# Banded attention followed by a ReLU-squared FFN on one core: earlier first load, other load order, pair-mask copies moved behind block 3

## Chip, cores, metric

The kernel runs on one core of one Trainium2 chip. The metric is the device time of one execution in microseconds; lower is better. All runs told here are of the state called fast; the kernel uses one core, so a slow die plays no part.

The names of the engines: PE is TensorE (PEld its loads of weights), DVE is VectorE, ACT ScalarE, POOL GpSimd and SP SyncE. "Clock" below is the share of PE's full clock that the trace shows as granted. A load "lands" when its data are on the chip.

## The reference, cut to what matters

```python
# q, k, v: (batch 8, heads 8, seq 576, head_dim 64) float32
scores = scale * q @ k.T                        # per batch and head
mask   = (rel >= 0) & (rel < 128)               # causal window of 128
scores = where(mask, scores + slope[h] * -abs(rel), -1e9)
attn   = softmax(scores);  a = attn @ v
x = a as (4608 tokens, 512)
h = x @ w_in                                    # 512 x 2048
out = maximum(h, 0) ** 2 @ w_out                # 2048 x 512
```

The 576 positions of a batch are cut into five blocks, four of 128 and one of 64 tokens, so there are 40 blocks, b0 to b39. A block's scores need its own keys and those of the block before it. 512 tokens make one FFN group, so group 0 is b0 to b3.

## The kernel before

The kernel is a planner. Each operation is added as a task with an engine, a sort key and its dependencies; the planner simulates the engines with rough durations and emits the instructions in the order that it finds. So moving one task can move others on all engines. On the chip each engine then works through its own list in that order.

The parts that the change touches are these; cuts are marked.

```python
FIRST = "b0 b1 b2 i0 i1 i2 b3 i3 o0 b4 b5 o1 b6 b7 o2 o3 b8 b9"   # order of loads: b block, i quarter of w_in, o quarter of w_out
KQ_PE = [0, 1, 2, 3, 4, 5, 6, 7, 8, 9]      # blocks whose k and q are transposed on PE; the others by DMA
WARM = 24                                    # dummy matmuls at the very beginning
FILL, UNTIL = 0.8, 26e3                      # share of planned PE gaps filled with dummy matmuls
...
t_iota = plan.add({"POOL": 360.0}, -9.1e5, build_iota)            # first on POOL, ahead of all loads
def build_ident():
    nc.vector.tensor_single_scalar(ident32, dist[:, 1], 0.0, op=ALU.is_equal)
    nc.vector.tensor_copy(ident, ident32)
...                                          # dist (DVE), then 8 masks (ACT)
def pair_rest():
    nc.vector.tensor_copy(pair_masks[:, :, 0:128].rearrange(...), masks[:, :, :, 0:64])
def pair_own():
    nc.vector.tensor_copy(pair_masks[:, :, 128:256], masks[:, :, 1, :])
t_pair = [plan.add({"DVE": 340.0}, -9e5 + 9, f, later + t_mask) for f in (pair_rest, pair_own)]
...
def load(key, ns, emit, deps=(), acq=()):
    return plan.add({"POOL": 900.0}, key, emit, deps, acq, dma=ns)   # issued by POOL, float32 in HBM to bf16 on chip
def load_w_in(n, key):                       # one quarter of w_in: 1 MB read, 512 KB written
    def emit():
        w = d_ff // 4
        nc.gpsimd.dma_start(w_in_sb[:, :, n * w:(n + 1) * w], moe_w_in[:, n * w:(n + 1) * w].rearrange(...))
    t_win[n] = load(key, 2550.0, emit)
...                                          # block 0's k and q: float32 through SP's queue; all else through POOL
```

The pair masks serve the bursts in which a 64-token block is taken together with the first block of the next batch; block 4 is the first of them. The dummy matmuls ("fillers") are there to keep PE busy, and so its clock up. Iota writes the table of distances from which the masks are built.

The softmax here doesn't subtract the row's maximum and nothing guards it: scores larger than these inputs give would overflow.

Of the kernel before, what the change touches and what calls it, by code (L numbers as in the profile page):

```python
# [38 lines left out]
class Plan:  # L39


    LAT = {"PE": 260.0, "ACT": 220.0, "DVE": 220.0, "POOL": 200.0, "SP": 2200.0}
    BEGIN = {"POOL": 1250.0}

    def __init__(self, bufs, pools, cold):
        self.tasks = []
# [124 lines left out]
def kernel(  # L171
    ctx: ExitStack, tc: tile.TileContext, q, k, v, moe_w_in, moe_w_out, out
):
    nc = tc.nc
# [12 lines left out]
    NG = NT // 512  # L187
    NBLK = B * NKB

    FIRST = "b0 b1 b2 i0 i1 i2 b3 i3 o0 b4 b5 o1 b6 b7 o2 o3 b8 b9"  # L190
    SPLIT = {0: [(0, 128), (128, 256), (256, 384), (384, 512)], 1: [(0, 192), (192, 512)]}
    EARLY = -80
    AHEAD = {10: -60, 1: 60, 4: 90, 9: -60, 5: -60, 0: -30, 12: 60, 11: 90, 2: 60, 8: 90, 7: 60, 6: 0, 3: -30, 24: 30, 14: 0, 18: 30, 25: 0, 23: 30, 16: -30, 13: 30, 21: 0, 19: -30}
    LEAD = 20

    KQ_PE = [0, 1, 2, 3, 4, 5, 6, 7, 8, 9]
    X_PE = [0, 1, 2, 3, 4, 5, 7, 8, 12, 17]
    WARM = 24
    FILL, UNTIL = 0.8, 26e3
    COLD = 0  # L200
    BANKS = {"A": 4, "B": 4}
    HOLD, OSB = 12, 14

# [17 lines left out]
        return [const.tile(shape, BF16, name=f"{name}_{i}") for i in range(n)]  # L221


    size = {"kq": 8, "v": 8, "kqT": 5, "P": 2, "x": 4}
    kq = ring("kq", size["kq"], [128, 2, d_model])
    vt = ring("vt", size["v"], [128, H, D + 1])
    kqT = ring("kqT", size["kqT"], [128, 2 * C, 128])
# [14 lines left out]


    def build_iota():
        nc.gpsimd.iota(dist, pattern=[[-128, 2], [1, 128]], base=128, channel_multiplier=-1,
                       allow_small_or_imprecise_dtypes=True)

    t_iota = plan.add({"POOL": 360.0}, -9.1e5, build_iota)

    def build_ident():  # L250
        nc.vector.tensor_single_scalar(ident32, dist[:, 1], 0.0, op=ALU.is_equal)
        nc.vector.tensor_copy(ident, ident32)

    t_ident = plan.add({"DVE": 350.0}, -9e5 - 1, build_ident, [t_iota])

    def build_dist():
        mid = (window - 1) / 2.0
# [16 lines left out]
                                 scale=-(2.0 ** (-8.0 * (h + 1) / H)))  # L274
        t_mask.append(plan.add({"ACT": act(256)}, -9e5 + h, build_mask, [t_dist]))

    later = []

    def pair_rest():
        nc.vector.tensor_copy(pair_masks[:, :, 0:128].rearrange("p h (t s) -> p h t s", t=2), masks[:, :, :, 0:64])  # L280

    def pair_own():
        nc.vector.tensor_copy(pair_masks[:, :, 128:256], masks[:, :, 1, :])  # L283

    t_pair = [plan.add({"DVE": 340.0}, -9e5 + 9, f, later + t_mask) for f in (pair_rest, pair_own)]

    def ones():
        nc.vector.memset(zero, 0.0)
# [26 lines left out]
    def load(key, ns, emit, deps=(), acq=()):  # L315
        return plan.add({"POOL": 900.0}, key, emit, deps, acq, dma=ns)

    t_win = [None] * 4
    t_wout = [None] * 4

    def load_w_in(n, key):
        def emit():
            w = d_ff // 4
            nc.gpsimd.dma_start(
                w_in_sb[:, :, n * w:(n + 1) * w],
                moe_w_in[:, n * w:(n + 1) * w].rearrange("(c p) f -> p c f", p=128))
        t_win[n] = load(key, 2550.0, emit)

    def load_w_out(n, key):
        def emit():  # L330
# [7 lines left out]
    def load_block(m, key):  # L338
        b, kb = divmod(m, NKB)
        n = blk[kb]  # L340
        wide = m == 0
        s_in[m, "k"] = s_in[m, "q"] = Slot("kq")
        s_in[m, "v"] = Slot("v")
        for i, (nm, src) in enumerate((("k", k), ("q", q), ("v", v))):
            sl = s_in[m, nm]
            if wide and nm != "v":
                def emit32(i=i, src=src):
                    nc.sync.dma_start(kq32[:, i].rearrange("s (h d) -> s h d", h=H),
                                      src[b, :, kb * 128:kb * 128 + n, :].rearrange("h s d -> s h d"))
                t_in[m, nm] = plan.add({"SP": 450.0}, key + 0.01 * i, emit32, dma=870.0)  # L350
                continue

            def emit(i=i, src=src, sl=sl, nm=nm):
                o = (vt[sl.idx][0:n, :, 0:D] if nm == "v"
                     else kq[sl.idx][0:n, i].rearrange("s (h d) -> s h d", h=H))
                nc.gpsimd.dma_start(o, src[b, :, kb * 128:kb * 128 + n, :].rearrange("h s d -> s h d"))  # L356
            deps = [t_ones] if nm == "v" else []
            if n < 128:
                deps.append(t_zeros.get("v" if nm == "v" else "kq"))
            t_in[m, nm] = load(key + 0.01 * i, 870.0 * n / 128, emit, deps, [sl])  # L360

    for i, what in enumerate(FIRST.split()):
        {"b": load_block, "i": load_w_in, "o": load_w_out}[what[0]](int(what[1:]), -9e5 + i)
# [24 lines left out]
    def turn(m):  # L388
# [12 lines left out]
        elif m == 0:  # L401
            t_kq = []
            for i in range(2):
                slot = Slot("B")
                last = None
                for c in range(C):
                    def emit(i=i, c=c, slot=slot):
                        nc.tensor.transpose(bank(slot)[:, c * 128:(c + 1) * 128],
                                            kq32[:, i, c * 128:(c + 1) * 128], ident32)
                    last = plan.add({"PE": mm(128)}, due - 56, emit,  # L410
                                    [last, t_ident, t_in[m, "kq"[i]]] + chain["tp"],
                                    ([slot] + ([sk] if i == 0 else [])) if c == 0 else [])
                chain["tp"] = [last]

                def evac(i=i, slot=slot):
                    copy(t_kq[i], kqT[sk.idx][:, i * C:(i + 1) * C, 0:n],
                         slot.tile.rearrange("p (c s) -> p c s", c=C)[:, :, 0:n])
                t_kq.append(plan.add({"ACT": act(C * n), "DVE": dve(C * n)}, due - 56, evac, [last], [], [slot]))
        else:
            slot = Slot("B" if first else "A")  # L420
            slot.turns = True
            last = None
            for i in range(2 * C):
                def emit(i=i):
                    nc.tensor.transpose(bank(slot)[:, i * 128:(i + 1) * 128],  # L425
                                        kq[s_in[m, "k"].idx][:, i // C, (i % C) * 128:(i % C + 1) * 128], ident)
                last = plan.add({"PE": mm(128)}, due - 56, emit,
                                [last, t_ident, t_in[m, "kq"[i // C]]] + ([t_in[m, "q"]] + chain["tp"] if i == 0 else []),
                                [slot, sk] if i == 0 else [], [s_in[m, "k"]] if i == 2 * C - 1 else [])
            chain["tp"] = [last]  # L430
            t_kq = []
            for i in range(2):
                def evac(i=i):
                    copy(t_kq[i], kqT[sk.idx][:, i * C:(i + 1) * C, 0:n],
                         slot.tile[:, i * 512:(i + 1) * 512].rearrange("p (c s) -> p c s", c=C)[:, :, 0:n])
                t_kq.append(plan.add(both if first else {("DVE", "ACT")[i]: both[("DVE", "ACT")[i]]},
                                     due - 56, evac, [last], [], [slot]))
# [3 lines left out]
    def score(ms):  # L441
# [6 lines left out]
        for i, m in enumerate(ms):  # L448
# [1 line left out]
            parts_of[m] = ([(0, m - 1)] if kb else []) + [(1, m)]  # L450
            P_of[m] = (sP, t_P)
            for part, mk in parts_of[m]:
                at = 128 * i + 64 * part if pair and i == 0 else 128 * part
                at_of[m, part] = at
                rel = [sk_of[mk]] if part == 0 or kb == NKB - 1 else []
                work_of.append((m, mk, n, at, rel))
        lo = min(w[3] for w in work_of)
        hi = max(w[3] + w[2] for w in work_of)
        n = 128 if pair else work_of[0][2]

        def burst():

            for sl in slot_s:
                bank(sl)
            for c in range(C):
                for m, mk, w, at, _ in work_of:
                    for half in range(2):
                        rows = slice(half * 64, half * 64 + 64)
# [2 lines left out]
                                :, c % 2, at:at + w],  # L471
                            kqT[sk_of[mk].idx][rows, c, :], kqT[sk_of[m].idx][rows, C + c, 0:w],
                            start=True, stop=True)
        tm = plan.add({"PE": 220.0 + C * sum(max(w[2], 64) / 2.4 + 4 for w in work_of)}, due - 28, burst,
                      [t for w in work_of for x in w[:2] for t in t_kq_of[x]] + chain["s"], slot_s + [sP],
                      [x for w in work_of for x in w[4]])
        chain["s"] = [tm]
        for i in range(4):
            def view(t):
                if pair:  # L480
                    return t
                return t.rearrange("p c (t q) -> p c t q", t=2)[:, :, lo // 128:2, 0:n]

            def Pv(i=i):
                return view(Pt[sP.idx][:, 2 * i:2 * i + 2].rearrange("p h t q -> p h (t q)"))

            def expo(i=i):
                nc.scalar.activation(Pv(i), view(slot_s[i].tile.rearrange("p (c x) -> p c x", c=2)),  # L488
                                     AF.Exp, bias=0.0, scale=scale)
            cols = 2 * sum(w[2] for w in work_of)  # L490
            te = plan.add({"ACT": act(cols)}, due - 28 + 3 * i, expo, [tm], [], [slot_s[i]])

            def mask(i=i):
                pt = Pv(i)
# [79 lines left out]
    while m < NBLK:  # L574
        ms = [m, m + 1] if m % NKB == NKB - 1 and m + 1 < NBLK else [m]
        for x in ms:
            turn(x)
        score(ms)
        for x in ms:
            mix(x)  # L580
        m += len(ms)
# [8 lines left out]
    def fc_step(g, unit, key, lo=0, hi=512):  # L590
# [10 lines left out]
        for fi, fc in enumerate(fcs):  # L601
            for cc in range(C):
                def emit(cc=cc, fc=fc, fi=fi):
                    nc.tensor.matmul(bank(slot)[:, fi * w:(fi + 1) * w], w_in_sb[:, cc, fc * 128:(fc + 1) * 128],  # L604
                                     xT[:, cc, g * 512 + lo:g * 512 + hi], start=cc == 0, stop=cc == C - 1)
                last = plan.add({"PE": mm(w)}, key + (fi * C + cc) * w / 512, emit,
                                [last, t_win[fc // 4]] + tokens(g * 512 + lo, g * 512 + hi),
                                [slot, sg] if cc == 0 and fi == 0 else [])
        srt = Slot("rt")

# [90 lines left out]
    def filler(slot, n):  # L701
        def emit():
            for i in range(n):
                if slot.turns:
                    nc.tensor.transpose(bank(slot)[:, 0:128], zero, ident)
                else:
                    nc.tensor.matmul(bank(slot)[:, 0:128], zero, zero, start=True, stop=True)  # L707
        t = Task({"PE": 107.0 * n / 2}, 0, emit, [t_ones, t_ident], [slot])
        t.eng, t.start, t.end, t.seq, t.cols = "PE", 0.0, 0.0, 0, 128 * n
        return t  # L710

# [47 lines left out]
```

## Time and profile before

The median was 312.97 us (312.77 to 313.3, 3 runs).

| reading | value | where |
|---|---|---|
| span | 311.3 us | page |
| chain that ended last, on PE | 95% | page, part 4 |
| first FFN matmul | 16.27 us | timeline |
| masks on ACT | 6.93 to 9.48 us | timeline |
| pair-mask copies on DVE | 9.52 to 11.07 us | timeline |
| quarter 0 of w_in lands | 14.8 us | DMA view (issue plus time to landing) |

From the page of the kernel before, its engine totals and its chain (part 4 gives shares of the span by engine, then by engine, tile and line):

```profile
PE 303.2 (97%) x2784; PEld 174.2 (56%) x2824; DVE 165.3 (53%) x482; ACT 179.2 (58%) x342; POOL 107.3 (34%) x134
...
PE 95%; ACT 1%; DVE 1%; issue 1%; DVEq 0%
PE B L604 40%; PE B L665 40%; PE A L469 6%; PE A L516 5%; PE A L311 1%; PE B L516 1%; ACT masks L273 1%; PE B L707 1%; PE A L425 1%; ACT kqT L375 1%; PE B L425 0%; DVE kqT L373 0%; PE A L562 0%; PE B L562 0%; DVE pair_masks L283 0%
```

L604 and L665 are the two FFN products. PE is the limit nearly everywhere, so the kernel is as long as the lost time at its begin plus PE's work. A caution: the page has 812 of 832 matmuls of L604 and 572 of 592 of L665, by the count of weight loads. PE looks idle where a record is missing, so the small idle times after 35 us are no real waits.

The timeline of the kernel before, single lines of the first 17 us (start, duration, engine, line, what, and in brackets the idle time before it and who ended that):

```profile
0.84 0.34 POOL L245 IOTA dist<- 128x256 f32 x1 [0.39 <-POOLq L743]
1.38 1.04 POOL L356 DMA_DIRECT2D vt<-in_v_dram  x1 [0.19 <-DVE vt L290]
...
5.34 1.06 PE L408 MATMUL B<-ident,kq 128*128 128x128 f32 x4
...
6.93 2.55 ACT L273 ACTIVATE masks<-dist 128x256 bf16<-128x256 f32 x8
7.63 2.31 POOL L324 DMA_DIRECT2D w_in_sb<-in_moe_w_in_dram  x3
...
9.52 0.67 DVE L280 COPY pair_masks<-masks 128x1024 bf16<-128x1024 bf16 x1 [1.14 <-ACT masks L273]
10.11 0.96 DVE L283 COPY pair_masks<-masks 128x1024 bf16<-128x1024 bf16 x1
...
16.27 1.06 PE L604 MATMUL B<-xT,w_in_sb 128*128 128x128 bf16 x16
```

The reader sees two things run side by side: the chain on chip (masks, pair copies, scores, softmax, x) and the queue of loads on POOL. The first FFN matmul needs both. When quarter 0 of w_in lands is read from the DMA view, restricted to the stretch in which it was issued (7.63 us); its last column is the time from issue to landing:

```profile
w_in_sb<-in_moe_w_in_dram POOLq DMA_DIRECT2D x1, 512.0 KB, 7.2
```

7.63 + 7.2 = 14.8 us. So in this execution the data waited about 1.4 us for the chain, not the chain for the data.

Up to about 7 us its PE works at half its later pace: block 0's k transposes take 1.06 us at 5.34 us. In the trace of e10_small_before (an experiment below, with the same instructions up to there) they are faster:

```profile
4.98 0.61 PE L408 MATMUL B<-ident,kq 128*128 128x128 f32 x4
```

In e8_extra_before, too, they took 0.61 us, at 5.28 us. The first FFN matmul was at 15.38 us in e10_small_before, and in e8_extra_before PE was free for it from 15.8 us. So up to 0.9 us of the 16.27 us, and of the slack of 1.4 us, belongs to this one execution. The clock column does not show it: it reads 1.00 from 1 to 8 us in all three traces.

### The profile page before, as it was taken

What the parts mean: (1) busy time and instruction counts of PE and PEld (TensorE: products, weight loads), DVE (VectorE), ACT (ScalarE), POOL (GpSimd) and SP (SyncE); (2) the same over time, 40 slices, a digit from 0 to 9 for tenths busy, and PEclk for the clock granted to TensorE, in tenths of its full rate; (3) what the DMA queues carried; (4) which work ended last, traced back from release to release, by engine and by line L of the source; (5) the groups of instructions that cost most, each with busy time, mean ns of one, the idle gap of its engine ahead of it and who ended that gap; (6) DMA issues with size and microseconds to landing.
All of it is one profiled execution on the core that took longest, in us unless ns stands there. A gap on an engine that the chain in (4) does not pass through costs nothing.

```text
span 311.3 us, 7139 instructions
## 1 busy us (share of the span) xinstructions
PE 303.2 (97%) x2784; PEld 174.2 (56%) x2824; DVE 165.3 (53%) x482; ACT 179.2 (58%) x342; POOL 107.3 (34%) x134
## 2 busy tenths in 40 slices
PE   8899999999999999999999999999999999999996
PEld 8799868675555555455454544445444454444443
DVE  4777666566557867676265555556455542222200
ACT  3777747585467847666455656665456654444411
POOL 8845958885546184365532120100000000000100
PEclk9999999999999999999999999999999999999999
DMA  9999999999999999999999994755422120000021
GB/s 133 181 190 179 173 181 158 167 156 149 148 147 164 144 115 153 134 171 151 210 180 165 134 200 118 137 127 103 128 87 84 53 59 34 37 34 35 34 97 73
DMA packets 168114, 39.86 MB, mean 128 GB/s; under 512 B 159440, under 2 KB 163792, under 8 KB 168080
## 3 DMA queue, kind: packets, MB, share of 16 engines
q0 software_dynamic: 114896, 18.88, 88.1%
q1 hardware_dynamic: 53184, 20.52, 33.5%
q8 instruction: 22, 0.36, 0.5%
q14 instruction: 12, 0.10, 0.1%
HBM read 36.70 MB, written 9.44 MB: 148 GB/s over the span
## 4 chain that ended last, share of the span: by engine, by line
PE 95%; ACT 1%; DVE 1%; issue 1%; DVEq 0%
PE B L604 40%; PE B L665 40%; PE A L469 6%; PE A L516 5%; PE A L311 1%; PE B L516 1%; ACT masks L273 1%; PE B L707 1%; PE A L425 1%; ACT kqT L375 1%; PE B L425 0%; DVE kqT L373 0%; PE A L562 0%; PE B L562 0%; DVE pair_masks L283 0%
## 5 line engine op out<-in xcount | busy, mean ns | idle before, releaser
L604 PE MATMUL B<-xT,w_in_sb 128*128 128x512 bf16 (+3 forms) x812 | 144.5, 312 | 1.7 <-issue 0.8
L665 PE MATMUL B<-w_out_sb,g 128*128 128x512 bf16 (+2 forms) x572 | 141.4, 373 | 1.3 <-issue 0.5
L613 ACT ACTIVATE rt<-B 128x512 bf16<-128x512 f32 (+2 forms) x152 | 86.6, 583 | 73.4 <-PE B L604 67.2
L620 DVE TENSOR_TENSOR g<-rt 128x512 bf16<-128x512 bf16 (+2 forms) x152 | 61.3, 406 | 73.5 <-ACT rt L613 72.4
L604 PEld LDWEIGHTS <-w_in_sb 128*128 128x128 bf16 x832 | 66.7, 98 | 48.0
L665 PEld LDWEIGHTS <-g 128*128 128x128 bf16 x592 | 54.2, 98 | 55.9
L488 ACT ACTIVATE P<-A 128x512 bf16<-128x512 f32 (+1 forms) x132 | 69.4, 589 | 19.2 <-PE A L469 19.2
L496 DVE TENSOR_TENSOR P<-P,masks 128x512 bf16<-128x512 bf16 (+1 forms) x104 | 42.4, 412 | 25.7 <-ACT P L488 22.3
L356 POOL DMA_DIRECT2D vt<-in_v_dram x40 | 34.3, 859 | 46.2 <-PE A L516 43.2
L356 POOL DMA_DIRECT2D kq<-in_k_dram x39 | 33.5, 859 | 44.7 <-DMA kqT<-kq 38.4
L356 POOL DMA_DIRECT2D kq<-in_q_dram x39 | 33.5, 860 | 6.5 <-DMA w_in_sb<-in_moe_w_in_dram 1.8
L636 ACT ACTIVATE osb<-B 128x512 f32<-128x512 f32 (+1 forms) x36 | 21.6, 600 | 23.9 <-PE B L665 23.9
L516 PEld LDWEIGHTS <-P 128*128 128x128 bf16 x576 | 26.8, 98 | 14.8 <-DVE P L496 0.5
L644 POOL DMA_DIRECT2D out_dram<-osb x3 | 1.7, 563 | 89.5 <-ACT osb L636 89.5
L544 DVE TENSOR_TENSOR x<-A,rec 128x256 bf16<-128x256 f32 (+1 forms) x70 | 28.8, 419 | 1.4
L516 PE MATMUL A<-vt,P 128*128 128x65 bf16 x504 | 25.7, 193 | 0.0
L469 PEld LDWEIGHTS <-kqT 64*128 64x128 bf16 x576 | 14.9, 94 | 12.9 <-issue 12.2
L469 PE MATMUL A<-kqT,kqT 64*128 64x128 bf16 (+1 forms) x256 | 17.8, 212 | 0.9 <-DVE kqT L373 0.8
L469 PE MATMUL A<-kqT 64*128 64x128 bf16 (+1 forms) x320 | 18.4, 211 | 0.0
L539 DVE RECIPROCAL rec<-A 128x4 f32<-128x4 f32 (+1 forms) x70 | 12.1, 179 | 11.6 <-PE A L516 10.8
L496 DVE TENSOR_TENSOR P<-P,pair_masks 128x512 bf16<-128x512 bf16 x28 | 11.7, 420 | 6.7 <-ACT P L488 5.6
L638 DVE COPY osb<-B 128x128 f32<-128x128 f32 x1 | 0.3, 291 | 13.7 <-PE B L665 13.7
(48 smaller groups left out, 82.6 us busy)
## 6 DMA issues: line engine op xcount, KB each, us to landing
out_dram<-osb SPq DMA_DIRECT2D x32, 256.0 KB, 2.3
vt<-in_v_dram POOLq DMA_DIRECT2D x32, 128.0 KB, 6.1
kq<-in_k_dram POOLq DMA_DIRECT2D x31, 128.0 KB, 6.2
kq<-in_q_dram POOLq DMA_DIRECT2D x31, 128.0 KB, 6.5
w_in_sb<-in_moe_w_in_dram POOLq DMA_DIRECT2D x4, 512.0 KB, 9.9
w_out_sb<-in_moe_w_out_dram POOLq DMA_DIRECT2D x4, 512.0 KB, 9.1
out_dram<-osb POOLq DMA_DIRECT2D x3, 256.0 KB, 2.4
kq<-in_k_dram POOLq DMA_DIRECT2D x8, 64.0 KB, 6.8
```

Source lines behind the costliest of these rows:

```text
L356: nc.gpsimd.dma_start(o, src[b, :, kb * 128:kb * 128 + n, :].rearrange("h s d -> s h d"))
L469: nc.tensor.matmul(slot_s[2 * (c // 2) + half].tile.rearrange("p (c x) -> p c x", c=2)[:, c % 2, at:at + w], kqT[sk_of[mk].idx][rows, c, : ...
L488: nc.scalar.activation(Pv(i), view(slot_s[i].tile.rearrange("p (c x) -> p c x", c=2)), AF.Exp, bias=0.0, scale=scale)
L496: nc.vector.tensor_tensor(pt, pt, view(mk), op=ALU.mult)
L516: nc.tensor.matmul(bank(slot_v)[:, hi * (D + 1):(hi + 1) * (D + 1)], Pt[sP.idx][:, place(h)].rearrange("p t q -> p (t q)")[:, at_of[m, par ...
L539: nc.vector.reciprocal(srec.tile[0:n, :], pv[0:n, :, D])
L544: nc.vector.tensor_tensor(xt[sx.idx][0:n, hf * 256:(hf + 1) * 256].rearrange("p (h e) -> p h e", h=4), pv[0:n, :, 0:D], srec.tile[0:n, :]. ...
L604: nc.tensor.matmul(bank(slot)[:, fi * w:(fi + 1) * w], w_in_sb[:, cc, fc * 128:(fc + 1) * 128], xT[:, cc, g * 512 + lo:g * 512 + hi], star ...
L613: nc.scalar.activation(srt.tile[:, 0:cols], slot.tile[:, 0:cols], AF.Relu, bias=0.0, scale=1.0)
L620: nc.vector.tensor_tensor(sg.tile[:, fcs[0]:fcs[-1] + 1, lo:hi], r, r, op=ALU.mult)
L636: nc.scalar.activation(so.tile[:, lo:hi], slot.tile[:, lo:hi], AF.Copy)
L665: nc.tensor.matmul(bank(slot)[:, lo:hi], sg.tile[:, fc, t * 128:(t + 1) * 128], w_out_sb[:, fc, lo:hi], start=fc == 0, stop=fc == FCB - 1)
```

## The change

Its intent is to begin dense PE work earlier. A load goes ahead of iota; block 1's k and q go ahead of block 0's v; the pair-mask copies leave the begin and follow block 3's mask multiplies; the second quarter of w_in comes as two loads (so i0 to i4 are five loads, and i4 is the last quarter); block 4 is loaded ahead of the last quarter of w_in. Besides: half the fillers, four more warm-up matmuls, block 9's k and q transposed by DMA instead of PE, one kq, one v and one x buffer fewer, other priorities. The code for "quarters" is new too but switched off (99).

```diff
-    FIRST = "b0 b1 b2 i0 i1 i2 b3 i3 o0 b4 b5 o1 b6 b7 o2 o3 b8 b9"
+    FIRST = "b0 b1 b2 i0 i1 i2 i3 b3 b4 i4 o0 b5 o1 b6 b7 o2 b8 o3 b9"
-    AHEAD = {10: -60, 1: 60, 4: 90, ... }
+    AHEAD = {10: -30, 1: 60, 4: 90, ... }          # (cut)
-    KQ_PE = [0, 1, 2, 3, 4, 5, 6, 7, 8, 9]
+    KQ_PE = [0, 1, 2, 3, 4, 5, 6, 7, 8]
-    WARM = 24
-    FILL, UNTIL = 0.8, 26e3
+    WARM = 28
+    FILL, UNTIL = 0.4, 26e3
+    V0 = 1
+    W_IN = [0, 4, 6, 8, 12, 16]                     # bounds of the w_in loads, in units of 128 columns
+    PAIR_AFTER, PAIR_KEY = 3, -100
-    size = {"kq": 8, "v": 8, "kqT": 5, "P": 2, "x": 4}
+    size = {"kq": 7, "v": 7, "kqT": 5, "P": 2, "x": 3}
-    t_iota = plan.add({"POOL": 360.0}, -9.1e5, build_iota)
+    t_iota = plan.add({"POOL": 360.0}, -9e5 + 1.005, build_iota)
+    t_ident16 = plan.add({"DVE": 230.0}, -9e5 + 1, build_ident16, [t_ident])    # bf16 copy, a task of its own
-    t_pair = [plan.add({"DVE": 340.0}, -9e5 + 9, f, later + t_mask) for f in (pair_rest, pair_own)]
+    t_pair = [plan.add({"DVE": n}, PAIR_KEY, f, t_mask) for n, f in ((670.0, pair_rest), (960.0, pair_own))]
-            t_in[m, nm] = load(key + 0.01 * i, 870.0 * n / 128, emit, deps, [sl])
+            t_in[m, nm] = load(key + 0.01 * i + V0 * (m == 0), 870.0 * n / 128, emit, deps, [sl])
+        if m == PAIR_AFTER:
+            for t in t_pair:
+                t.deps += P_of[m][1]
 ... (cut: the two halves of the mask tile swapped, the quarters code that is off, t_win by 128-column piece, some of the planner's rough durations)
```

## The prediction

> **What bounds the kernel now.** TensorE. The chain of waits puts 95% of the 311.3 us span on PE, 80% in the two FFN matmul groups. The stage table has PE busy 262.15 of 265 us between 35 and 300 us. So time is saved only by less PE work, an earlier begin of dense PE work, or a shorter tail.
>
> The change aims at the begin. The timeline shows the first FFN matmul at 16.27 us. Before it the chain of waits holds only about 4.5 us of real PE work. About 12 us are lost: 24 warm-up matmuls (2.74 us), fillers, ACT masks (2.46 us, 7.04 to 9.5), two pair-mask copies on DVE (0.67 + 0.96 us, 9.52 to 11.07), evictions. After 16.27 us fillers cost about 0.6 us.
>
> **Landings in before** (issue plus time to landing, DMA view): block 0 k 3.95 us, q 5.2; block 1 k 6.8, q 7.8; w_in quarter 0 14.8, quarter 1 16.5, quarter 2 19; block 3 20.7 to 23; quarter 3 25. Block 0's k is transposed at 5.34, behind 17 cold fillers (119 ns each); q at 7.04, behind 9 more. Fillers delay the chain.
>
> **What the change does, costed.**
> 1. POOL's first load begins at about 0.85 us instead of 1.38; later ones gain 0.3 us. Block 1's k, q land 1.3 us earlier; block 0's v about 1.3 us later, at 7.5 us, still early enough (P times v began at 12.2).
> 2. Ident comes about 0.9 us later, hidden behind the k load. I expect ACT to build the masks from about 4.5 us, before block 0's evictions, which go to DVE.
> 3. The pair copies (1.63 us) leave the chain and return on DVE near 28 us, where it is 94% busy (3.75 of 4 us, 26 to 30), but off the critical path if the rt buffers absorb them.
> 4. Half the fillers, 4 more warm-up matmuls (0.45 us).
> 5. Together: scores of block 1 at 9.5 to 10.5 us instead of 11.65, block 0's x 3 us earlier. Then the first FFN matmul waits for w_in quarter 0, at about 14.5 us: gain 1.2 to 1.7 us, not 3.
> 6. Part is given back: the last w_in quarter now follows block 4, at an estimated 26 us or later instead of 25. Three quarters on three blocks are 8.1 us of FFN work, done near 24 us. I charge 0.6 us.
> 7. Block 9 turns k, q by DMA: 8 PE transposes (0.45 us) less, full gain. One fewer kq and x buffer: POOL and SP wait more, PE doesn't.
> 8. The tail is unchanged.
>
> Sum: 1.4 - 0.6 + 0.45 + 0.3 (fewer fillers, earlier loads) = about 1.6 us. **Predicted 311.3 us; 309.7 to 312.9 should hold it 8 times in 10. Faster by over 2%: 3%; within 2%: 96%; slower: 1%.**
>
> **What would show it.** Right: first FFN matmul between 14.3 and 15.2 us, directly after w_in's landing; masks on ACT before 7 us; pair copies after 25 us with no PE gap; gap or fillers of 0.3 to 1.2 us on PE between 23 and 27 us; 64 bf16 k, q transposes instead of 72. Wrong: the first FFN matmul stays near 16 us, or PE idles over 1.5 us later.
>
> **What would make it wrong.** The PE clock: the Trainium skill, "TensorE: Matmul & The Clock Gate", Part 1, says that activity over a free-running window of about 3.4 us releases the clock. Here 128-column matmuls take 107 to 119 ns each until about 7 us, 6 us after the first, and 56 ns afterwards. With half the fillers, release may come a window later: about +1 us. Starvation at 23 to 28 us may eat all the gain; or the earlier begin may pay in full (another 1 us).

## More of the kernel before

Times scatter, though: the unchanged kernel before ranged from 312.13 to 313.92 us over all jobs. Differences of a few tenths of a microsecond are therefore not told from two single runs. The jobs also ran on different chips, and before's median was 312.87, 313.02, 313.01, 312.66 and 312.71 us in them; times of different jobs are best compared through their ratios to before. In the execution of the timeline before, which has a late warm-up, the data of quarter 0 waited about 1.4 us for the chain (14.8 to 16.27 us), not the chain for the data.

## The result, and the profile after

The changed kernel took 313.42 us in the median (313.07 to 313.63, 4 runs) against 312.87 us (312.38 to 313.3, 4 runs). The ratio is 1.0017, 95% interval 0.9999 to 1.0035. Ratios here and below are the mean time of one kernel's fast runs over that of the other's of the same rounds, so not quite the ratio of the quoted medians. A later job repeated it: 313.19 against 312.71 us, ratio 1.0025 (1.0006 to 1.0044). The predicted gain of 1.6 us was not there; the measured time lies above the stated range of 309.7 to 312.9.

From the page of the kernel after, its engine totals and the head of its chain:

```profile
PE 304.7 (98%) x2765; PEld 171.9 (55%) x2765; DVE 165.6 (53%) x482; ACT 178.3 (57%) x339; POOL 108.7 (35%) x136
...
PE 91%; DMA 6%; POOL 2%; issue 0%; DVE 0%; POOLq 0%; DVEq 0%
PE B L697 40%; PE B L636 39%; PE A L490 5%; PE A L545 5%; DMA kq<-in_q_dram 4%; DMA w_in_sb<-in_moe_w_in_dram 2%; POOL kq L363 1%; POOL vt L363 1%; PE A L433 1%; PE B L545 0%; PE A L591 0%; PE B L591 0%; PE B L433 0%; POOL dist L249 0%; DVE osb L670 0%
```

PE gives up 4 points of the chain, and DMA and POOL, which had none, take 8. Followed back, the chain now reaches the begin through the landing of block 4's q and of w_in, no longer through masks and pair copies.

The timeline of the kernel after, the lines that answer to those of before:

```profile
1.27 1.04 POOL L363 DMA_DIRECT2D kq<-in_k_dram  x1 [0.82 <-POOLq L775]
2.40 0.37 POOL L249 IOTA dist<- 128x256 f32 x1
...
5.12 2.56 ACT L281 ACTIVATE masks<-dist 128x256 bf16<-128x256 f32 x8 [3.09 <-DVE dist L269]
7.94 3.04 POOL L332 DMA_DIRECT2D w_in_sb<-in_moe_w_in_dram  x4
...
15.06 1.85 PE L636 MATMUL B<-xT,w_in_sb 128*128 128x128 bf16 x16 [1.27 <-DMA w_in_sb<-in_moe_w_in_dram]
15.30 0.69 POOL L363 DMA_DIRECT2D kq<-in_q_dram  x1 [1.01 <-DMA w_in_sb<-in_moe_w_in_dram]
...
30.41 0.40 DVE L287 COPY pair_masks<-masks 128x1024 bf16<-128x1024 bf16 x1
31.06 0.42 DVE L290 COPY pair_masks<-masks 128x1024 bf16<-128x1024 bf16 x1
```

(L636 is the line of the first FFN product after the change, L697 that of the second.) The chain on chip is indeed earlier: masks 1.8 us earlier, no pair copies at the begin. The first FFN matmul is at 15.06 instead of 16.27 us. (These are single traces, and before's had the late warm-up: against e10_small_before's masks, at 6.12 us, the lead is 1.0 us.) But the bracket names what it waits for now: the landing of w_in, with PE wholly idle for 1.27 us. And the 16 matmuls take 1.85 us, where the same 16 took 1.06 us before. The same landing holds up POOL: it issues block 4's q at 15.30 us, 0.3 us after the landing, having waited 1.01 us for it by the profile. Why POOL waits the trace does not show, but a later quarter 0 makes the loads behind it later, too.

Why the 16 matmuls are slow is shown by the stage table of PE, one microsecond a line (length, busy time and count of PE, granted clock, DMA share, GB/s; the DMA share adds up the times of all packets and can pass 1). After:

```profile
14.00:15.00 1.00, 0.00 (x0) 1.00 1.42 189
15.00:16.00 1.00, 0.94 (x10) 0.57 1.45 195
16.00:17.00 1.00, 1.00 (x12) 0.50 1.34 202
17.00:18.00 1.00, 1.00 (x13) 0.50 1.26 208
18.00:19.00 1.00, 1.00 (x19) 0.72 1.47 192
...
25.00:26.00 1.00, 0.53 (x16) 1.00 1.29 199
26.00:27.00 1.00, 0.88 (x13) 1.00 1.26 209
```

The clock is at half from about 15 to 18.5 us in this execution. At 25 to 27 us PE is idle again, for 0.6 us; the list of waits names the landing of block 4's k and q. In before these stretches have clock 1.00, and PE is busy from 25 to 27 us throughout.

How much FFN work is done by when is counted from the weight loads, of which no record is missing. The stage table for the weight loads of the first FFN product, before (busy time and count, clock, DMA share, GB/s):

```profile
0.00:20.00 20.00, 2.62 (x46) 1.00 1.52 164
20.00:30.00 10.00, 8.08 (x144) 1.00 1.84 183
```

and after:

```profile
0.00:20.00 20.00, 3.75 (x46) 0.91 1.48 159
20.00:30.00 10.00, 6.57 (x116) 1.00 1.87 172
```

In these two traces after begins 1.2 us earlier, and at 20 us it has done no more: 46 matmuls of the first product in both, so the lead is gone by then. From 20 to 30 us it does 28 fewer. At 56 ns each (16 take 0.89 us in the chain of waits before) that is 1.57 us; it has done 8 transposes more (0.45 us) in their place, those of block 4.

From 35 to 300 us both are dense, and the tail has the same form. Stage table of all engines, columns PE, weight loads, DVE, ACT, POOL, clock, DMA share, GB/s, before:

```profile
35.00:300.00 265.00, 262.15 (x2179) 138.63 (x2215) 142.29 (x409) 155.21 (x293) 82.21 (x100) 1.00 1.21 125
```

after:

```profile
35.00:300.00 265.00, 265.00 (x2236) 138.96 (x2235) 142.63 (x409) 155.20 (x293) 83.30 (x102) 1.00 1.27 125
```

(The counts, 2179 against 2236 matmuls, fit the records that are missing in before; so the 2.85 us less in its busy time are taken for those, not for waits.) So the difference arises before 35 us.

### The profile page after: what moved, and what is told of

Same layout as the page of the kernel before. It is cut to its first block, busy times and chain, and to the rows that moved or that the text cites. A ratio compares the mean times of both kernels' runs of the same rounds, so it can differ in the third digit from the quotient of the medians.

```text
span 311.8 us, 7072 instructions
## 1 busy us (share of the span) xinstructions
PE 304.7 (98%) x2765; PEld 171.9 (55%) x2765; DVE 165.6 (53%) x482; ACT 178.3 (57%) x339; POOL 108.7 (35%) x136
## 2 busy tenths in 40 slices
DMA packets 169633, 40.11 MB, mean 129 GB/s; under 512 B 160512, under 2 KB 165376, under 8 KB 169600
## 4 chain that ended last, share of the span: by engine, by line
PE 91%; DMA 6%; POOL 2%; issue 0%; DVE 0%; POOLq 0%; DVEq 0%
PE B L697 40%; PE B L636 39%; PE A L490 5%; PE A L545 5%; DMA kq<-in_q_dram 4%; DMA w_in_sb<-in_moe_w_in_dram 2%; POOL kq L363 1%; POOL vt L363 1%; PE A L433 1%; PE B L545 0%; PE A L591 0%; PE B L591 0%; PE B L433 0%; POOL dist L249 0%; DVE osb L670 0%
## 5 line engine op out<-in xcount | busy, mean ns | idle before, releaser
L636 PE MATMUL B<-xT,w_in_sb 128*128 128x512 bf16 (+3 forms) x832 | 149.3, 316 | 1.3 <-DMA w_in_sb<-in_moe_w_in_dram 1.3
L697 PE MATMUL B<-w_out_sb,g 128*128 128x512 bf16 (+2 forms) x592 | 145.4, 373 | 0.0
L636 PEld LDWEIGHTS <-w_in_sb 128*128 128x128 bf16 x832 | 68.0, 99 | 49.3 <-DMA w_in_sb<-in_moe_w_in_dram 1.4
L697 PEld LDWEIGHTS <-g 128*128 128x128 bf16 x592 | 54.3, 98 | 56.1
```

The costliest lines, as they stand in the source:

```text
L636: nc.tensor.matmul(bank(slot)[:, fi * w:(fi + 1) * w], w_in_sb[:, cc, fc * 128:(fc + 1) * 128], xT[:, cc, g * 512 + lo:g * 512 + hi], star ...
L697: nc.tensor.matmul(bank(slot)[:, lo:hi], sg.tile[:, fc, t * 128:(t + 1) * 128], w_out_sb[:, fc, lo:hi], start=fc == 0, stop=fc == FCB - 1)
```

## The experiments

Two theories stood after these traces. **Clock**: the idle microsecond drops the clock, and running at half speed until 18.5 us eats the gain. **Supply**: at the begin the loads set the pace, so that whatever the chain on chip gains is spent waiting for data. The second has variants: the last w_in quarter (at 28.7 us), POOL's issuing, or the bytes that go ahead of quarter 0. Every kernel was timed in five rounds against before on the same chip (e1 to e4 in one job, e5 to e8, e9 to e12 and r1 to r4 in three others). Each left one trace, of its first run. "After" in the edits is the changed kernel.

| run | edit | median us (lowest to highest) | before, same job | ratio (95%) |
|---|---|---|---|---|
| e1_warm | dummies ahead of first FFN matmul | 313.09 (312.16 to 314.20) | 313.02 | 1.0005 (0.9983 to 1.0027) |
| e2_quarter3 | last quarter ahead of b4 | 313.34 (311.75 to 315.48) | 313.02 | 1.0021 (0.9983 to 1.0058) |
| e3_both | both | 313.06 (312.09 to 313.65) | 313.02 | 1.0003 (0.9985 to 1.0021) |
| e4_iota | iota first again | 313.18 (312.40 to 314.76) | 313.02 | 1.0012 (0.9988 to 1.0036) |
| e5_free_after | w_in by memset, after | 310.22 (309.92 to 310.70) | 313.01 | 0.9917 (0.9903 to 0.9931) |
| e6_free_before | w_in by memset, before | 320.25 (320.24 to 320.88) | 313.01 | 1.0236 (1.0221 to 1.0250) |
| e7_extra_after | 512 KB more, after | 316.47 (314.72 to 317.53) | 313.01 | 1.0111 (1.0087 to 1.0135) |
| e8_extra_before | 512 KB more, before | 314.87 (314.53 to 316.29) | 313.01 | 1.0073 (1.0054 to 1.0092) |
| e9_small_after | w_in loads cut, after | 310.07 (309.74 to 310.31) | 312.66 | 0.9918 (0.9904 to 0.9931) |
| e10_small_before | w_in loads cut, before | 312.31 (311.69 to 313.04) | 312.66 | 0.9988 (0.9974 to 1.0002) |
| e11_pair_early | pair copies early again | 313.39 (312.78 to 315.90) | 312.66 | 1.0033 (1.0006 to 1.0061) |
| e12_wide | b1's k, q through SP | 312.70 (311.98 to 313.42) | 312.66 | 1.0000 (0.9984 to 1.0015) |
| r1_after | after, unchanged | 313.19 (312.88 to 314.73) | 312.71 | 1.0025 (1.0006 to 1.0044) |
| r2_both | e3_both again | 312.77 (311.62 to 314.45) | 312.71 | 1.0003 (0.9981 to 1.0024) |
| r3_cut_first | only quarter 0 cut | 311.06 (310.51 to 311.48) | 312.71 | 0.9944 (0.9931 to 0.9956) |
| r4_cut_last | only last quarter cut | 313.25 (312.20 to 314.78) | 312.71 | 1.0020 (0.9995 to 1.0045) |

### e1_warm: keep the clock up

```diff
+            if t is first_ffn[0]:
+                out.append(filler(t.acq[0], 22))     # 22 dummy matmuls just ahead of the first FFN matmul
```

> The kernel after, with 22 dummy matmuls put directly before the first FFN matmul, so that PE is busy in the 1.27 us in which it waits for w_in quarter 0. Clock theory: half clock from 15.06 to about 18.5 us cost 1.7 us; with it gone the time falls by 1.2 to 1.7 us, to about 312.0. Supply theory: the last w_in quarter lands at 28.7 us and all FFN work that is possible without it is done by 28.6; the clock stays full, but the time falls by at most 0.5 us (312.9 to 313.4) and PE idles that much longer between 25 and 29 us.

Measured 313.09 us. The clock stayed at 0.999 or more in all six runs. The drop is gone. Against before of the same job the time is 1.0005, after's was 1.0017 and, repeated, 1.0025: 0.4 to 0.6 us better, with intervals that overlap. That is less than the 1.2 to 1.7 us that the clock theory asked for, so the clock is not where the predicted 1.6 us went. In its trace PE is again idle for 0.27 us of the stretch 26 to 27 us, waiting at block 4. The clock theory as the main cause of the missing gain falls. The wait for quarter 0 itself moved: it landed at 15.8 us here instead of 15.0, although it was issued at the same 7.95 us.

Does the drop cost anything at all? After and r1_after together have ten runs: the four with clock 0.999 or more average 313.14 us, the six with less 313.73 us. That is 0.6 us more in the runs that have it. It need not all be the clock's cost: a late landing can bring about both the drop and a longer time. The dummies point to a similar size: the three jobs with them (e1_warm, e3_both, r2_both, 18 runs) are on average 0.1 us slower than before of their jobs, after's ten runs 0.7 us, each with a standard error of 0.2 us. Two of the three have another load order as well. So the drop may be most of the half microsecond by which after is slower than before, but not the gain that is missing.

### e2_quarter3 and e3_both: the last quarter earlier

```diff
-    FIRST = "b0 b1 b2 i0 i1 i2 i3 b3 b4 i4 o0 ..."
+    FIRST = "b0 b1 b2 i0 i1 i2 i3 b3 i4 b4 o0 ..."
```

> The kernel after, with the load of the last w_in quarter ahead of block 4's instead of behind it. Supply theory: it lands near 25.5 us instead of 28.7, PE has FFN work through 25 to 29 us, time falls by 0.6 to 1.2 us even though the clock still drops at 15 us in some runs. Clock theory: no change over 0.3 us.

> Both edits at once. Supply and clock as two limits in a row: with the quarter earlier the saved clock time is no longer waited away, so the two together give 1.8 to 2.7 us (310.8 to 311.6), more than the sum of the two alone. If the gains are independent: the sum. If block loads are the limit instead: under 0.8 us.

Both miss. e2_quarter3 took 313.34 us, not 0.6 to 1.2 us less; in its trace the last quarter landed only at 27.4 us, not at 25.5. Half of its runs had the drop of the clock; those average 314.59 us, the others 312.45; three runs of each kind are few. e3_both, with the dummies, took 313.06 us where 310.8 to 311.6 was expected. In its one trace (312.09 us) the last quarter landed at 25.8 us, the clock was full and PE never idle from 25 to 30 us, but its other runs were slower by 0.8 to 1.6 us and left no trace. One of them still shows a clock of 0.995, so the dummies do not always prevent the drop.

### e4_iota: iota ahead of the loads again

```diff
     done = fill(plan.order())
+    done.remove(t_iota)
+    done.insert(0, t_iota)
```

> The kernel after, with iota moved back ahead of the first load, all else in the same order. In after the first load began at 1.27 us only, 0.1 us earlier than before, and iota then held up all the later ones by 0.37 us. If that is so: first load still near 1.3 us, w_in quarter 0 lands 0.2 to 0.4 us earlier (14.7), time -0.2 to -0.5 us or nothing where the last quarter is the limit. If loads ahead of iota help, as the change intends: time +0.2 or more.

The first load began at 1.38 us (1.27 in after) and quarter 0 was issued at 7.71 us (7.94), as expected: the load ahead of iota saves 0.1 us for itself and delays all others by 0.2 us. But quarter 0 landed at 16.6 us in this trace, later than in after, not earlier. So a quarter of a microsecond at the issue is lost in the scatter of the landing, and the time (313.18 us) does not tell the two apart. PE was wholly idle for 2.85 us before the first FFN matmul here; the clock was still full then and fell to half from 18 us on.

### e5_free_after and e6_free_before: w_in without loads

```diff
-            nc.gpsimd.dma_start(w_in_sb[:, :, lo:hi], moe_w_in[:, lo:hi].rearrange(...))
+            nc.gpsimd.memset(w_in_sb[:, :, lo:hi], 0.01)      # wrong result on purpose
```

> Wrong result on purpose: the kernel after with every w_in load replaced by a memset of the same columns at the same place in the queue, so w_in is there by about 10 to 12 us and all later loads land earlier; the instruction order is otherwise that of after. Supply theory (the begin of after is set by when loads land): first FFN matmul at about 12.5 to 13.8 us instead of 15.06, no wait on a load between 24 and 29 us, no drop of the clock, time 2 to 3.5 us under that of after (310 to 311.4). If the saturated stretch, not the begin, is the limit: under 0.8 us.

> The same in the kernel before (wrong result on purpose). Supply theory: before is bound at its begin by its own chain (masks, pair copies, evictions), not by w_in, so it gains less than after does: first FFN matmul still at 15.5 to 16.3 us, time lower by 0.3 to 1.5 us (311.5 to 312.7). After without loads is then at least 1 us faster than before without loads: the on-chip part of the change is worth that. Rival (the on-chip part is worth nothing): the two are equal within 0.3 us.

e5_free_after took 310.22 us, 3.2 us under after and inside the expectation, though its first FFN matmul was at 14.09 us, slightly later than expected. e6_free_before failed as an experiment: it took 320.25 us. Two lines of its timeline show why:

```profile
4.14 9.00 DVE L260 TENSOR_SCALAR far<-far 128x256 f32<-128x256 f32 x1
...
7.62 5.37 POOL L324 MEMSET w_in_sb<- 128x2048 bf16 x3
```

The same instruction took 0.29 us in before. It ends at 13.14 us, just after the third memset (7.62 + 5.37 = 12.99). In after the dist chain on DVE is over by 5.1 us, before the memsets begin. The Trainium skill, "SBUF — State Buffer", section "SBUF: two separate sides", says that DVE operations in a 2-port mode and GpSimd operations share one port pair as an exclusive lock: whichever starts first has it for the whole instruction, and the other fully blocks. The trace agrees in where the stall ends, but not in where it begins: the DVE instruction stands from 4.14 us, 3.5 us before the first memset, while POOL was still issuing loads. Whether the lock is the cause of the whole stall, this run does not show. The pair can't be compared, so it was replaced by e9 and e10.

### e7_extra_after and e8_extra_before: one load more

```diff
+            if n == 0:      # 512 KB into a scratch tile that nothing reads, just ahead of quarter 0
+                nc.gpsimd.dma_start(scratch, moe_w_in[:, 0:d_ff // 4].rearrange(...))
```

> The kernel after with one more load of 512 KB (w_in's first quarter into a scratch tile that nothing reads) directly ahead of quarter 0. Supply theory: everything behind it lands 2 to 2.5 us later and the whole of it shows: first FFN matmul at 17 to 17.6 us, time +1.8 to +2.5 us against after (315.2 to 316). Otherwise: under +0.8 us.

> The same extra load in the kernel before. Supply theory: before has about 1.4 us between landing (14.8) and first use (16.27) of quarter 0, so a part is absorbed: first FFN matmul at 16.8 to 17.5 us, time +0.6 to +1.6 us (313.6 to 314.6). If before is as load-bound as after: +1.8 to +2.5 us. If not load-bound at all: under +0.4 us.

After loses 3.0 us (316.47 - 313.42, across jobs with nearly the same before), before loses 1.9 us (314.87 - 313.01). Both sizes are above the expected ones. Their order is as expected, but the intervals are too wide to tell the two losses apart. In after quarter 0 landed at 17.2 us and the first FFN matmul came at 17.28; all six runs had the drop of the clock. In before quarter 0 landed at 17.9 us, which is 3.1 us later than without the extra load, and the first FFN matmul came at 17.93, only 1.7 us later than without it. In the traces the slack between the landing and the first use absorbed the rest, and then before, too, waited for its loads (2.10 us on PE).

### e9_small_after and e10_small_before: a quarter of the bytes

```diff
-            nc.gpsimd.dma_start(w_in_sb[:, :, lo:hi], moe_w_in[:, lo:hi].rearrange(...))
+            nc.gpsimd.dma_start(w_in_sb[:, :, lo:lo + 128], moe_w_in[:, lo:lo + 128].rearrange(...))
-                    nc.tensor.matmul(..., w_in_sb[:, cc, fc * 128:(fc + 1) * 128], ...)
+                    nc.tensor.matmul(..., w_in_sb[:, cc, base(fc) * 128:(base(fc) + 1) * 128], ...)   # base: first piece of that load
```

The result is wrong; the number and order of the instructions and the shapes of the matmuls are unchanged. The pages of after and e9_small_after count the same 169633 DMA packets, so it is bytes, not packets, that are fewer.

> Wrong result on purpose, in place of the memset run (there DVE stood still while POOL filled memory): the kernel after, each w_in load cut to its first 128 columns, and the FFN matmuls of that quarter all read those; same instructions in the same order, but 2.6 of 4.2 MB less to read, or so, before block 4. Supply theory: the wait for quarter 0 goes, first FFN matmul at 13.5 to 14.0 us, later stalls on block 4 go, 310.0 to 311.2 us, that is 2 to 3.3 us under after. Rival (after loses its time on chip, in clock or order): less than 1 us under after.

> The same cut in the kernel before (wrong result on purpose). Supply theory: before's begin is bound by its own chain through masks and pair copies, first FFN matmul at 15.8 to 16.3 us, time 311.8 to 312.8 us, at most 1.2 us under before; so without the loads as a limit the change would be worth 1 to 2.5 us. Rival (both are bound by loads alike, the change's work on the chain is worth nothing): before gains as much as after, within 0.5 us.

This is the run that decides. After fell to 310.07 us, before only to 312.31 us. Both times are inside the expectation; before's first FFN matmul, at 15.38 us, came earlier than the 15.8 to 16.3 expected. The first FFN matmuls, from the timeline of e9_small_after:

```profile
13.58 1.06 PE L640 MATMUL B<-xT,w_in_sb 128*128 128x128 bf16 x16
```

and of e10_small_before:

```profile
15.38 1.06 PE L604 MATMUL B<-xT,w_in_sb 128*128 128x128 bf16 x16
```

Neither waits for data: quarter 0 landed at 12.2 and 12.7 us. So the chain on chip allows 13.58 us after the change and 15.38 us before it, a gain of 1.80 us; both traces have the early warm-up. With 0.45 us for the eight transposes less that makes 2.25 us; the times differ by 312.31 - 310.07 = 2.24 us. That close an agreement is luck (one trace each, and runs that scatter by up to 1.35 us), the size is not. Without the w_in bytes the change does what it was meant to do, and the full w_in loads take all of it back: with them it is 0.5 us slower than before, not 2.24 us faster.

The scatter of the changed kernel shrinks as well: 309.74 to 310.31 us for e9_small_after, 312.88 to 314.73 us for r1_after. That of e10_small_before (311.69 to 313.04 us) does not shrink against before's, so this alone proves nothing.

### e11_pair_early: the pair copies back at the begin

```diff
-    t_pair = [plan.add({"DVE": n}, PAIR_KEY, f, t_mask) ...]
+    t_pair = [plan.add({"DVE": n}, -9e5 + 9, f, t_mask) ...]
-    PAIR_AFTER, PAIR_KEY = 3, -100
+    PAIR_AFTER, PAIR_KEY = None, -100
```

> The kernel after with the two pair-mask copies back behind the masks, ahead of block 0's mask multiplies. Supply theory: block 0's x comes 0.5 to 1.6 us later (ready by 13 to 14 us), but still before quarter 0 lands at 15 to 15.8, so first FFN matmul and time are those of after within 0.4 us (313.0 to 313.8). Chain theory (the copies were on the critical path): +1.0 to +1.6 us.

313.39 us, the time of after. The copies ran from 7.86 to 9.01 us and block 0's x was on its way to the FFN by 13.1 us; the first FFN matmul waited for quarter 0 until 15.61 us all the same. With the loads as they are, moving the pair copies is worth nothing measurable.

### e12_wide: fewer issues on POOL

```diff
-        wide = m == 0
+        wide = m in (0, 1)          # block 1's k and q, too, in float32 through SP's queue, turned by float32 transposes
```

> An attempt at a better version: block 1's k and q, too, are loaded in 32 bits on SP's queue (idle then) and turned by 32-bit transposes, so POOL has two loads less to issue (0.87 us each) ahead of w_in. Supply theory: quarter 0 is issued at about 6.2 us instead of 7.94 and lands 0.8 to 1.7 us earlier (13.4 to 14.3 us), time 0.8 to 1.8 us under after (311.6 to 312.6). If the DMA engines and not POOL's issuing limit the first 8 us: landing and time the same as after within 0.4 us.

On the landing the rival wins. Quarter 0 was issued 2.04 us earlier and landed at the same time. The line of e12_wide's timeline in which its w_in loads begin, then the DMA view's line for quarter 0, in e12_wide and in after:

```profile
5.90 3.02 POOL L333 DMA_DIRECT2D w_in_sb<-in_moe_w_in_dram  x4
```

```profile
w_in_sb<-in_moe_w_in_dram POOLq DMA_DIRECT2D x1, 512.0 KB, 9.1
```

```profile
w_in_sb<-in_moe_w_in_dram POOLq DMA_DIRECT2D x1, 512.0 KB, 7.1
```

5.90 + 9.1 = 15.0 us; in after 7.94 + 7.1 = 15.0 us. So POOL's issuing did not set the landing; the transfers on the DMA engines are what is left. (They were not quite the same: in float32 block 1's k and q write 256 KB each instead of 128.) The Trainium skill, "DMA: Bandwidth & Descriptors", section "Issuing engines are not separate DMA queues", says that transfers from all issuing engines run on the same 16 DMA engines and that issuing from several at once only saves the sequencer's time. This run agrees: 2.04 us of issue time saved, 0.0 us at the landing. The time, 312.70 us, does not test the supply theory as it was meant to, because the landing was not what the first FFN matmul waited for in this trace:

```profile
10.64 0.66 PE L416 MATMUL B<-ident,kq 128*128 128x128 f32 x4 [1.53 <-DMA kq<-in_q_dram]
...
16.71 1.33 PE L637 MATMUL B<-xT,w_in_sb 128*128 128x128 bf16 x21
```

Block 1's q came late, the clock was at half from 12 to 15 us, and the first FFN matmul followed 1.7 us after the landing, later than in after. Still the time equals before's, and by the ratios it is 0.5 to 0.8 us under after's, with intervals that overlap. It beats neither clearly, and it shows that the time of the first FFN matmul alone does not decide.

### r1_after, r2_both, r3_cut_first, r4_cut_last: where the bytes count

r1_after is the changed kernel and r2_both is e3_both, both unedited. The other two use the cut of e9 for one load only:

```diff
+            hi2 = lo + 128 if n in (0,) else hi          # r3_cut_first; (4,) in r4_cut_last
```

> The kernel after once more, unchanged, beside the others of this job, for a second trace and the spread of its runs. Supply theory: landing of w_in quarter 0 and of the last quarter shifts by up to a microsecond from run to run and the time with it; median 313.0 to 313.6.

> The kernel with the last quarter ahead of block 4 and the dummies once more: its first trace had a span of 310.3 us, its other five runs 311.1 to 311.9. If the place of the last quarter matters for itself: at least 0.6 us under the unchanged after of this job. If only the sum of the loaded bytes matters: within 0.4 us of it.

> Wrong result on purpose: after with only quarter 0's load cut to 128 columns (1 MB to 0.25 MB of reads, some 1.9 us of transfer); every later load then comes that much earlier. Supply theory by bytes: nearly the gain of all five cuts, first FFN matmul at about 13.6 us, time 1.3 to 2.2 us under after. Last-quarter theory (what comes before 20 us is waited away again at 25 to 29 us): the last quarter still comes 1.5 us earlier, so the same; told apart from it by the next run.

> Wrong result on purpose: after with only the last quarter's load cut likewise; the begin (quarter 0 at 15 us, drop of the clock in some runs) stays, quarter 3 lands at about 27 us instead of 28.7. Last-quarter theory (step 6 of the prediction, larger than charged): at least 1.0 us under after. Begin theory (only what comes before the first FFN matmul counts): under 0.4 us. Supply by bytes: 0.4 to 1.2 us.

r3_cut_first: 311.06 us, 2.1 us under r1_after. Quarter 0 landed at 13.1 us, the first FFN matmul was at 14.27 without a wait for data (later than the expected 13.6), and the clock was 0.999 or more in all runs. One load cut, 0.75 MB less to read, gives two thirds of what all five cuts give (r1_after to e9: 3.1 us). The time is inside the expectation. POOL issued block 4's q at 14.16 us, without the wait for quarter 0 that it has in after (15.30 us) and r1_after (15.88 us).

r4_cut_last: 313.25 us, no gain. In its trace the last quarter landed at 25.8 us, as early as in e3_both and 2 to 3 us earlier than in after (28.7) and r1_after (28.0), and nothing came of it. PE was still late from the begin. Its first FFN matmul:

```profile
15.53 1.07 PE L641 MATMUL B<-xT,w_in_sb 128*128 128x128 bf16 x16 [1.86 <-DMA w_in_sb<-in_moe_w_in_dram]
```

So the last quarter, where the prediction placed the loss, is not by itself the limit; quarter 0 is, with what comes behind it. The cut of r3_cut_first brings every later load forward by about two microseconds, too, so it does not say that only the first landing counts.

r1_after fell within its expectation and its trace repeats the first one: quarter 0 at 15.6 us, an idle PE before it (1.97 us), clock 0.50 until 18 us. Its first FFN matmul, at 15.64 us, is only 0.6 us ahead of before's trace. r2_both was 0.4 us under r1_after in the median, and their intervals overlap. The order of the loads for itself is left undecided at that size. Its traced run was again its fastest (311.62 us), with quarter 0 at 14.7 us; why ten other runs of the same two kernels were slower, these data do not show.

No correct kernel beat before clearly. The best medians, 312.70 (e12_wide) and 312.77 us (r2_both), equal before's 312.66 and 312.71 us of the same jobs.

## Why the prediction was wrong, point by point

- **What bounds the kernel** (PE, dense after 35 us): right. The stretch from 35 to 300 us stayed dense, and the loss lies before it.
- **Point 1** (first load at 0.85 us, later ones 0.3 us earlier): wrong. POOL's first load began at 1.27 us although nothing was ahead of it, so iota had been in a gap of its own before. With iota behind it the later loads were issued 0.3 us later (7.94 instead of 7.63 us). That cost little: in e12_wide an issue 2.04 us earlier did not move the landing. Block 1's k and q did land earlier, by 1.1 and 0.9 us (1.3 predicted).
- **Points 2 and 3** (masks before block 0's evictions, pair copies later without harm): right. Masks ran from 5.12 us, expected from 4.5. The copies ran at 30.41 and 31.06 us with no gap on PE, and took 0.40 and 0.42 us there instead of 0.67 and 0.96.
- **Point 5** (then quarter 0 sets the first FFN matmul; 14.3 to 15.2 us): right in place and cause, 15.06 us, directly after the landing. The size was partly luck: 1.2 us in that pair of traces, but r1_after's 15.64 us lies outside the range, and before's 16.27 us had the late warm-up.
- **Point 7** (8 transposes less): 64 bf16 transposes of k and q by the group view, 72 before. The 0.45 us fits the sum of e9 and e10, but was not tried alone; nor were the fillers (point 4) or the smaller buffers.
- **The step that failed** is point 6, "I charge 0.6 us", and with it the sum. Its place was wrong: it put the give-back at the last w_in quarter, and with that quarter landing at 25.8 us instead of 28.0 to 28.7 nothing was gained (r4_cut_last). Its size was wrong: in the two traces the whole lead of 1.2 us was gone by 20 us, at the wait for quarter 0 and the half clock after it, and by 30 us another 1.1 us (28 FFN matmuls less, 8 transposes more), part of it at the wait for block 4. The give-back was therefore about 2.3 us, four times the charge. 1.2 + 0.45 - 2.3 = -0.65 us, against a measured loss of 0.5 us in the spans (311.8 and 311.3).
- **Why it was mis-sized.** The prediction treated the begin as a gain and the supply as a small later charge at the last quarter. The runs show the supply as the limit of the whole begin: quarter 0 landed at 14.7 to 16.6 us in all traces of after's family with full w_in loads and no load added, whatever was issued when. Without that limit the change is worth 2.24 us (e9 against e10), and cutting quarter 0 alone gives 2.1 us (r3_cut_first). The prediction had the landing time of before (14.8 us) but took it as fixed and as slack, without asking for its scatter.
- **The clock**: named as a risk, but at the warm-up near 7 us. The warm-up was fine: the float32 transposes of block 0 already took 0.61 us at 5.3 us. In the traces of after and r1_after the drop came right after the wait for quarter 0, in e4_iota and r4_cut_last one to two microseconds after it. 6 of 10 runs of after have a clock below 0.999, and they are 0.6 us longer. It goes with the same wait, and curing it (e1_warm) does not bring the gain.

What stays open: how after's loss of 0.5 us with full loads splits between the drop of the clock, the wait at block 4 and the later landings; why POOL does not issue block 4's q before quarter 0 has landed; and why the traced runs of e3_both and r2_both are the fastest of their kernels.

## What to carry to other kernels

When two chains meet, here work on chip and a queue of loads, shortening one is worth no more than the slack of the other; test the other chain directly by cutting its bytes with a wrong result, in both kernels, before costing the gain. A begin that waits on loads also takes over their scatter, and PE can lose its clock there on top, as in 6 of after's 10 runs. An earlier issue need not be an earlier landing: in e12_wide 2.04 us at the issue were worth 0.0 us at the landing. And one trace of a kernel is one execution: compare the warm-up of two traces before taking their difference for the change's.

## What the Trainium skill lacked or had wrong

- "TensorE: Matmul & The Clock Gate", section "Why this matters for your kernels", advises to avoid PE-idle gaps over about 3 us because one idle window brings the half clock back. Here the clock fell to half after a wholly idle stretch of only 1.27 us (after) or 1.97 us (r1_after), with PE partly idle before it (busy 1.49 of 2 us from 12 to 14 us in after). In e2_quarter3's trace PE waited 1.80 us without a drop. In e4_iota's it waited 2.85 us, and the half clock came only from 18 us on, when PE had been at work again for 1.3 us. So that row's 3 us are no safe bound; what decides whether the drop comes, these traces do not show.
- The same page, Part 1, gives about 4 us of sustained activity for warm-up, give or take half a microsecond. The trace before shows 128-column matmuls at 107 to 119 ns until about 7 us, 6 us after the first, with PE busy throughout. In e8_extra_before and e10_small_before, whose instructions are the same up to there, transposes ran at full pace by 5.28 and 4.98 us, about 4 us after the first. The scatter was thus about 2 us.
- "SBUF — State Buffer", section "SBUF: two separate sides": the exclusive lock is stated, but no page gives a size for a DVE operation that stands still while several GpSimd operations run in a row. Here one DVE instruction of 0.29 us took 9.00 us, until three memsets of 5.37 us in all were through; 3.5 us of it lay before them.
- No page tells how much a landing scatters from run to run. Here the same 512 KB load, issued at 7.95 us behind the same loads, landed between 14.7 and 15.8 us in the traces of after, r1_after, e1_warm, e2_quarter3, e3_both, r2_both and r4_cut_last.
